# Block-sparse attention into a gated MLP: spatial weights cast in parts, and casts, loads, transposes and splits put elsewhere in the order

## The chip, the cores and the metric

The kernel runs on one core of a Trainium2 chip. The metric is the device time of one execution in microseconds (us); before the change it was 218.19 us, the median of three runs (216.72 to 219.64). The profile is one execution of 218.0 us, with a span of 216.2 us from its first to its last instruction. TensorE had its full clock throughout.

## The reference, cut to what matters

Attention for 4 batches of 8 heads, 768 positions of 64 elements each, under a mask of 32 x 32 blocks (neighbours, first and last blocks, and three sampled ones for each row of blocks). The heads of a batch are joined to rows of 512 and go through a gated MLP whose gate mixes positions by a 768 x 768 matrix, the spatial weights.

```
scores = scale * q @ k.T              # masked by blocks of 32
attn   = softmax(scores)
x      = (attn @ v), heads joined     # [4, 768, 512]
h      = relu(x @ w_in)               # [4, 768, 1024]
u, v   = h[..., :512], h[..., 512:]
v_n    = (v - mean(v)) / sqrt(var(v) + 1e-6)
v_s    = einsum('ts,bsd->btd', w_spatial, v_n) + b_spatial
out    = (u * v_s) @ w_out
```

## The kernel before

**Pairs and slots.** Two heads make a pair; there are 16 pairs (0 to 15), four to a batch. The order of all work is written out by hand, in slots. A slot does one chunk of scores and its exponential: two TensorE matmuls of 384 columns and one ScalarE exponential of 128 x 768. Slots 0 to 47 (`for g in range(N0)`, L672) are batch 0's four pairs, in halves of the queries (`qk_exp_half`, L386, matmuls L396). Then the loop over `p` from 4 to 16 (L728) runs twelve slots `s` for each pair, `g = 12 * p + s` (`qk_exp`, L356, matmuls L361, exponential L365). Behind each slot's scores come one or more matmuls of the MLP (`moe_q.popleft()()`, all through L520) and, seven slots behind the scores, one chunk of attention times values (`av`, L370, matmuls L377; `av_half` with L412 in batch 0). A head that is through is divided by its sums on VectorE (`rc` L442, `xn` L443; L423 and L424 in batch 0) and transposed for the MLP: by a DMA (`xtr`, L466), in batch 0 by TensorE (L433) with a VectorE copy to `xt` (L434).

**What a pair needs.** For pairs from 4 on, `load(p)` (L107) brings q, k and v as floats into `st_q`, `st_k`, `st_v`, two buffers each. `prepare(p)` (L147) casts k, q and v to bf16 on POOL, in that order: `nat_k` and `nat_q` (L140), `vv` (`cast_v`, L143). `tr_dma` (L342, L344) transposes `nat_k` and `nat_q` by DMA into `tt_k` and `tt_q`. `split_pair(p, "k")` and `split_pair(p, "q")` (L347, L350) copy the two heads' halves with VectorE into `kt_all` and `qt_all`, from where the scores read them: two copies of 64 x 768 bf16 for each split. Pair `p`'s splits stand in the slots of pair `p - 1`, its casts and transposes in those of `p - 2`, its loads in those of `p - 3`.

**Queues.** Each engine does its instructions in the order in which this code issues them, and waits for what the instruction at its head needs. All loads, the transposes, and nearly all stores are issued by one DMA queue, SyncE's, in program order too.

**The MLP.** `moe_units(b)` makes the list of a batch: for each of six row chunks, v (`v_post`: relu into `vsb` L533, statistics L536 and L537) and u (`u_post`, L554 or L557); then the mixing product (L520, reading `w_spt` and `vn`; `s_post` makes `gn`, L586, and transposes it by DMA, L590), then the product with `w_out`. After each third v chunk POOL makes `std` (L540) and `rstd` (L542) from the means and variances `mv`, and VectorE then makes `vn` (`normalize`, L547) one chunk at a time, in slots given by `norm_q`. A product's PSUM tile is one of two banks in turn, which its `post` frees.

**The spatial weights.** They come as three loads of 128 x 2 x 768 floats (`load_weights`, L170) and are cast by `cast_weights` (L180, L183) on POOL into `ws_nat`: one instruction for a load, in slot 28 of batch 0, two of them ahead of the loads and weight transposes listed there and one between. In `ws_nat` the order is by chunk, so the cast reads its source with a step of six floats. Six DMA transposes (`wspt`, L472) make `w_spt` of it.

## Time and profile before

| What | Value |
|---|---|
| Time, median of 3 | 218.19 us |
| Span of the profile | 216.2 us |
| Spatial weight casts (L183 POOL) | 3 of 2.97 us, 29.2 to 38.0 us |
| Split copies to `kt_all` (L350 VectorE) | 24, median 356 ns, longest 1929 ns |
| Split copies to `qt_all` (L350 VectorE) | 24, median 355 ns, longest 947 ns |
| POOL waiting for loads of k (L140) | 64.2 us in 11 waits, longest 13.4 us |
| Pair 6's k and q transposes issued | 54.01 and 55.33 us |
| Pair 7's loads issued | 50.28 to 51.76 us |
| Pair 7's k and q transposes issued | 58.20 and 59.52 us |
| Pair 10's loads issued | 83.96 to 85.56 us |
| First product with `w_out` | 82.3 us |

Reading it: a row of a group gives the line of the kernel, the engine, the operation, the tiles by name, and the mean duration; behind it the idle time of that engine before these instructions and what ended it. A row of a timeline gives start and length in us, then the same names, and in brackets the idle time just before it. The chain of waits follows the execution back from its last instruction to whatever released each step. The durations of TensorE's matmuls are modelled, and those of POOL are rough.

The scores of batch 0 run to about 43 us, pair 4's from 42.92 us, pair 5's from about 52 us, pair 6's from 63.87 us. The other pairs follow at 11 to 12 us each, and from about 188 us only batch 3's MLP is left.

### The profile page before, as it was taken

How to read it: one execution, taken by the hardware profiler on the slowest of the kernel's cores; microseconds unless marked ns; L12 is line 12 of the kernel's file. 1: busy time of each engine (PE TensorE's matmuls, PEld its weight loads, DVE VectorE, ACT ScalarE, POOL GpSimd, SP SyncE). 2: the span in 40 equal slices, each digit the busy share in tenths (PEclk: the TensorE clock that was granted, in tenths of full speed). 3: DMA queues.
4: the chain of work that ended last, by engine and by line, in shares of the span. 5: the costliest groups of instructions: out<-in, count | busy, mean ns of one | idle time of the engine just before them, and what ended most of it. 6: DMA issues, size and time to landing. Idle time of an engine off the chain costs nothing.

```text
span 216.2 us, 5234 instructions
## 1 busy us (share of the span) xinstructions
PE 205.8 (95%) x2065; PEld 125.7 (58%) x2099; DVE 132.0 (61%) x311; ACT 172.4 (80%) x238; POOL 69.4 (32%) x97
## 2 busy tenths in 40 slices
PE   8899999999979999999999999999899999999993
PEld 7567766566646666655566565655465656544441
DVE  6777949967454546356957463446978444585542
ACT  7899999899978999998899888888789885266031
POOL 6767979801626121402342400400502000022000
PEclk9999999999999999999999999999999999999999
DMA  5999999979989999999979448989712124620246
GB/s 142 318 338 385 394 325 290 192 125 275 273 229 282 151 244 188 257 287 302 196 181 212 106 83 241 234 168 297 145 19 39 25 52 86 219 101 0 58 120 234
DMA packets 64936, 42.24 MB, mean 195 GB/s; under 512 B 46896, under 2 KB 60560, under 8 KB 64912
## 3 DMA queue, kind: packets, MB, share of 16 engines
q1 hardware_dynamic: 64624, 41.58, 76.2%
q8 instruction: 16, 0.26, 0.5%
q10 hardware_dynamic: 288, 0.33, 0.5%
q14 instruction: 8, 0.07, 0.2%
HBM read 24.38 MB, written 6.29 MB: 142 GB/s over the span
## 4 chain that ended last, share of the span: by engine, by line
PE 82%; DVE 9%; DMA 3%; issue 2%; POOL 1%; ACT 1%; SPq 0%; ACTq 0%; DVEq 0%; POOLq 0%
PE ps_moe L520 32%; PE ps L361 20%; PE ps_av L377 12%; PE ps L396 6%; PE ps_av L412 4%; PE ps_t L520 3%; PE ps_sc L520 3%; DVE kt_all L350 2%; DMA st_k<-in_k_dram 2%; DVE vsb L533 2%; DMA out_dram<-osb 1%; DVE kt_all L277 1%; DVE osb L610 1%; PE ps_av L433 1%; PE ps_moe L322 1%
## 5 line engine op out<-in xcount | busy, mean ns | idle before, releaser
L365 ACT ACTIVATE a_all<-ps 128x768 bf16<-128x768 f32 x144 | 113.4, 813 | 16.5 <-PE ps L361 10.2
L361 PE MATMUL ps<-qt_all,kt_all 88*128 88x384 bf16 x288 | 70.4, 325 | 1.4 <-DVE qt_all L350 1.4
L377 PEld LDWEIGHTS <-a_all 128*128 128x128 bf16 x864 | 46.1, 97 | 34.0 <-issue 1.6
L377 PE MATMUL ps_av<-vv,a_all 128*128 128x65 bf16 x864 | 50.8, 194 | 0.3
L520 PE MATMUL ps_moe<-w_in_t,xt 128*128 128x512 bf16 x143 | 45.2, 378 | 1.9 <-DVE vsb L533 1.0
L400 ACT ACTIVATE a_all<-ps 128x768 bf16<-128x768 f32 x48 | 35.7, 812 | 2.6 <-PE ps L396 2.2
L140 POOL CAST nat_k<-st_k 128x768 bf16<-128x768 f32 (+1 forms) x14 | 10.9, 779 | 73.9 <-DMA st_k<-in_k_dram 64.2
L520 PE MATMUL ps_moe<-vn,w_spt 128*128 128x512 bf16 x110 | 33.1, 379 | 0.3
L586 DVE SCALAR_TENSOR_TENSOR gn<-ps_moe,b_col,un 128x512 bf16<-128x512 f32 x20 | 15.0, 750 | 21.5 <-PE ps_moe L520 17.9
L520 PEld LDWEIGHTS <-xt 128*128 128x128 bf16 x192 | 18.6, 97 | 15.3 <-issue 1.0
L396 PE MATMUL ps<-qt_all,kt_all 88*128 88x384 bf16 x96 | 23.4, 325 | 0.8 <-ACT a_all L400 0.2
L520 PE MATMUL ps_moe<-w_out_t,gt 128*128 128x512 bf16 x73 | 21.5, 378 | 0.3
L520 PEld LDWEIGHTS <-w_spt 128*128 128x128 bf16 x144 | 13.8, 97 | 11.6
L361 PEld LDWEIGHTS <-kt_all 88*128 88x128 bf16 x288 | 19.0, 98 | 2.0 <-DVE qt_all L350 1.5
L412 PEld LDWEIGHTS <-a_all 128*128 128x128 bf16 x288 | 14.9, 98 | 6.3 <-issue 0.9
L533 DVE TENSOR_SCALAR vsb<-ps_moe 128x512 bf16<-128x512 f32 x18 | 12.3, 682 | 10.1 <-PE ps_moe L520 10.0
L536 DVE BATCH_NORM_STATS2 stats<-vsb 128x6 f32<-128x512 bf16 x24 | 16.6, 694 | 1.5 <-ACT vsb L531 0.8
L412 PE MATMUL ps_av<-vv,a_all 128*128 128x65 bf16 x288 | 17.1, 194 | 0.4 <-DVE xt L434 0.4
L540 POOL TENSOR_SCALAR std<-mv 128x3 f32<-128x3 f32 x8 | 1.9, 242 | 42.0 <-DVE mv L537 30.6
L610 DVE COPY osb<-ps_moe 128x512 f32<-128x512 f32 x10 | 6.9, 690 | 13.3 <-PE ps_moe L520 9.8
L443 DVE TENSOR_TENSOR xn<-ps_av,rc 128x384 bf16<-128x384 f32 x24 | 13.4, 557 | 0.8
L520 PEld LDWEIGHTS <-gt 128*128 128x128 bf16 x96 | 8.8, 97 | 7.1
(100 smaller groups left out, 213.1 us busy)
## 6 DMA issues: line engine op xcount, KB each, us to landing
out_dram<-osb SPq DMA_DIRECT2D x23, 256.0 KB, 3.3
st_v<-in_v_dram SPq DMA_DIRECT2D x14, 384.0 KB, 5.5
st_k<-in_k_dram SPq DMA_DIRECT2D x13, 384.0 KB, 4.6
st_q<-in_q_dram SPq DMA_DIRECT2D x12, 384.0 KB, 3.5
wst<-in_moe_w_spatial_dram SPq DMA_DIRECT2D x3, 768.0 KB, 9.4
wst<-in_moe_w_in_dram SPq DMA_DIRECT2D x4, 512.0 KB, 7.7
wst<-in_moe_w_out_dram SPq DMA_DIRECT2D x2, 512.0 KB, 6.3
st_q<-in_q_dram SPq DMA_DIRECT2D x4, 192.0 KB, 6.2
```

The source lines that it names most:

```text
L140: eng.tensor_copy(out=dst, in_=src)
L361: nc.tensor.matmul(out=ps[:, hf * 512:hf * 512 + HALF], lhsT=kt[j % H][:, ci * 128:(ci + 1) * 128], rhs=qt[j % H][:, hf * HALF:(hf + 1) * ...
L365: nc.scalar.activation(out=a_ref[j][:, ci, :].rearrange("p (b c) -> p b c", b=2), in_=ps.rearrange("p (b c) -> p b c", b=2)[:, :, 0:HALF], ...
L377: nc.tensor.matmul(out=av_ref[j][:, qc, :], lhsT=a_ref[j][:, ci, qc * 128:(qc + 1) * 128], rhs=vv[p % NG][:, h, ci, :], start=(ci == 0), s ...
L396: nc.tensor.matmul(out=ps[:, u * 512:u * 512 + HALF], lhsT=kt[j][:, ci * 128:(ci + 1) * 128], rhs=qt[j][:, grp * HALF:(grp + 1) * HALF], s ...
L400: nc.scalar.activation(out=a_ref["half", gh][:, 2 * i:2 * i + 2, :], in_=ps.rearrange("p (b c) -> p b c", b=2)[:, :, 0:HALF], func=AF.Exp, ...
L412: nc.tensor.matmul(out=av_ref["half", gh][:, qc, :], lhsT=a_ref["half", gh][:, ci, qc * 128:(qc + 1) * 128], rhs=vv[p][:, h, ci, :], start ...
L443: nc.vector.tensor_tensor(out=xn_ref[p][:, :, h, :], in0=ps[:, :, 0:D], in1=rc.to_broadcast([128, NCH, D]), op=ALU.mult)
L520: nc.tensor.matmul(out=box[0], lhsT=lhs, rhs=rhs, start=(i == 0), stop=(i == n - 1))
L533: nc.vector.tensor_scalar(out=vsb[:, tcc, :], in0=ps, scalar1=0.0, scalar2=None, op0=ALU.max)
L536: nc.vector.bn_stats(out=stats, in_=vsb[:, tcc, :])
L586: nc.vector.scalar_tensor_tensor(out=gn[:, tcc, :], in0=ps, scalar=b_col[:, tcc:tcc + 1], in1=un[:, tcc, :], op0=ALU.add, op1=ALU.mult)
```

## The change

It moves work in the hand-written order and leaves the computation alone.

1. The three spatial casts are cut into six parts each, of 2 of 6 chunks of one of the two rows: 18 instructions of 128 x 256. VectorE and POOL can then take turns in smaller steps.
2. Pair 4's q split moves from slot 45 to slot 41, which puts its two copies directly behind those of k on VectorE. Pair 5's v cast moves from slot 42 to slot 53 (`p == NG`, `s == 5`), on POOL from ahead of the first `std` and `rstd` to behind them.
3. Around pairs 6 and 7: pair 7's loads go from `s` 9 to 11 of pair 4, so that pair 6's transposes (`s` 10, as before) stand ahead of them in the DMA queue. Pair 6's splits go from `s` 7 and 10 to 6 and 8 of pair 5. Pair 7's casts go from `s` 1 to 7 and its transposes from `s` 6 to 9 of pair 5; on POOL the second `std` and `rstd` now come ahead of them. Pair 8's loads and the two `w_out` loads behind them go from `s` 7 to 10 of pair 5. On the DMA queue, pair 4's `xt` transpose now stands ahead of pair 7's transposes.
4. Pair 10's loads go from `s` 7 to 10 of pair 7, behind a `gt` and an `xt` transpose.
5. Pair 14's splits go from `s` 7 and 10 to 5 and 6 of pair 13: all four copies then stand ahead of a head's `rc` and `xn` on VectorE.

The lists of instructions of TensorE and ScalarE stay as they are.

```diff
             if len(dst.shape) == 4:
                 t = t.rearrange("p a (s c) -> p a c s", c=NCH)
-            w_staged.append((t, dst))
+                w_staged.append([(t[:, i, c:c + 2], dst[:, i, c:c + 2])
+                                 for i in range(2) for c in range(0, NCH, 2)])
+            else:
+                w_staged.append([(t, dst)])
 
     def cast_weights(n):
         for _ in range(n):
-            t, dst = w_staged.popleft()
-            nc.gpsimd.tensor_copy(out=dst, in_=t)
+            for t, dst in w_staged.popleft():
+                nc.gpsimd.tensor_copy(out=dst, in_=t)
...
-        if g in (36, 42):
-            cast_v(4 if g == 36 else 5)
-        if g in (39, 45):
+        if g == 36:
+            cast_v(4)
+        if g in (39, 41):
             split_pair(4, "k" if g == 39 else "q")
...
     for p in range(NG, NP + 1):
+        change = NG < p < NP and p % NG == 0
+
+        splits = {NG: (3, 6), NG + 1: (6, 8), NP - 3: (5, 6)}.get(p, (7, 10))
+        s_prep = {NG: 7, NG + 1: 7}.get(p, 1)
+        s_tr = {NG: 10, NG + 1: 9}.get(p, 8 if change else 6)
+        s_load = {NG: 11, NG + 1: 10, NG + 3: 10}.get(p, 9 if change else 7)
         for s in range(12):
             g = 12 * p + s
-            change = NG < p < NP and p % NG == 0
...
-            if p + 1 < NP and s in ((3, 6) if p == NG else (7, 10)):
-                split_pair(p + 1, "k" if s in (3, 7) else "q")
-            if s == (10 if p == NG else 8 if change else 6) and p + 2 < NP:
+            if p + 1 < NP and s in splits:
+                split_pair(p + 1, "k" if s == splits[0] else "q")
+            if p == NG and s == 5:
+                cast_v(5)
+            if s == s_prep and p + 2 < NP:
+                prepare(p + 2)
+                if p == NG + 2:
+                    cast_weights(2)
+            if s == s_tr and p + 2 < NP:
                 tr_dma(p + 2, "k")
                 tr_dma(p + 2, "q")
-            if s == (7 if p == NG else 1) and p + 2 < NP:
-                prepare(p + 2)
-                if p == 6:
-                    cast_weights(2)
-            if s == (9 if change else 7) and p + 2 < NP:
-                if p + 3 < NP:
-                    load(p + 3)
-                if p == 5:
+            if s == s_load and p + 3 < NP:
+                load(p + 3)
+                if p == NG + 1:
                     load_weights(2)
```

## The prediction

> **What bounds the kernel now.** I read the page's first part, then the chain that ended last, then the timelines of single engines wherever TensorE waited. First the busy times, one engine to a line:
>
> ```profile
> PE 205.8 (95%) x2065; PEld 125.7 (58%) x2099; DVE 132.0 (61%) x311; ACT 172.4 (80%) x238; POOL 69.4 (32%) x97
> PE 82%; DVE 9%; DMA 3%; issue 2%; POOL 1%; ACT 1%; SPq 0%; ACTq 0%; DVEq 0%; POOLq 0%
> ```
>
> TensorE is busy for 205.8 of 216.2 us and holds 82% of the chain. The change leaves TensorE's and ScalarE's lists of instructions as they are, so it can only win time in which TensorE stands still. The start (about 1 us and the first load) and the last output transfer are untouched. Of the rest, TensorE's timeline shows three waits of more than 0.3 us behind VectorE; the bracket is the idle time and what ended it:
>
> ```profile
> 40.88 0.35 PE L412 MATMUL ps_av<-vv,a_all 128*128 128x65 bf16 x6 [0.38 <-DVE xt L434]
> 63.87 0.50 PE L361 MATMUL ps<-qt_all,kt_all 88*128 88x384 bf16 x2 [1.41 <-DVE qt_all L350]
> 154.26 0.59 PE L520 MATMUL ps_moe<-w_in_t,xt 128*128 128x512 bf16 x2 [0.77 <-DVE vsb L533]
> ```
>
> Together 2.56 us. By the starts, instead of the modelled ends, they are somewhat longer. Six L377 matmuls take 0.19 us in the chain, two L361 0.33 us. So TensorE was through at 62.10 + 0.19 = 62.29, and the second wait is 63.87 - 62.29 = 1.58 us. The third is 154.26 - (153.01 + 0.33) = 0.92 us, the first about 0.58 us (VectorE's release at 40.88, the weight load idle for 0.60). This 3.1 us, 1.4% of the time, is what the change can aim at.
>
> The first wait, in the timelines of POOL and VectorE (start, length, instruction), and two pieces of the chain:
>
> ```profile
> 35.02 2.96 POOL L183 CAST ws_nat<-wst 128x1536 bf16<-128x1536 f32 x1
> 36.27 2.30 DVE L350 COPY kt_all<-tt_k 64x768 bf16<-64x768 bf16 x2
> 38.48 0.17 DVE L423 RECIPROCAL rc<-ps_av 128x3 f32<-128x3 f32 x1
> 36.35 1.84 DVE kt_all L350
> 38.21 0.35 DVE kt_all L350
> ```
>
> The same copy takes 0.35 us or 1.9, and the long one ends 0.2 us after POOL's cast. The reciprocal had its input by 37.4 and starts at 38.48. All VectorE work behind it is about 1.1 us late, and TensorE meets that at 40.88.
>
> The second wait:
>
> ```profile
> 57.35 0.83 POOL L140 CAST nat_k<-st_k 128x768 bf16<-128x768 f32 x1 [1.13 <-DMA st_k<-in_k_dram]
> 58.89 0.83 POOL L143 CAST vv<-st_v 128x768 bf16<-128x768 f32 x1
> 59.81 0.23 POOL L540 TENSOR_SCALAR std<-mv 128x3 f32<-128x3 f32 x1
> 61.05 0.41 DVE L547 TENSOR_SCALAR vn<-vsb,mv,rstd 128x512 bf16<-128x512 bf16 x1 [3.12 <-POOL rstd L542]
> 63.47 0.73 DVE L350 COPY qt_all<-tt_q 64x768 bf16<-64x768 bf16 x2
> ```
>
> The statistics mv are there at 57.92, but POOL has pair 7's three casts ahead of std. VectorE idles 3.12 us at its first vn, and pair 6's splits stand behind that vn in its queue.
>
> The third wait:
>
> ```profile
> 151.68 0.83 POOL L140 CAST nat_q<-st_q 128x768 bf16<-128x768 f32 x1
> 152.45 0.95 POOL L143 CAST vv<-st_v 128x768 bf16<-128x768 f32 x1
> 151.79 1.82 DVE L350 COPY kt_all<-tt_k 64x768 bf16<-64x768 bf16 x2
> 153.53 0.67 DVE L533 TENSOR_SCALAR vsb<-ps_moe 128x512 bf16<-128x512 f32 x1
> ```
>
> Pair 14's two k copies take 0.84 and 0.88 us by the chain, each until a POOL cast is over; the vsb behind them frees the bank that TensorE wants.
>
> [...] The trace agrees: 1.84 us beside the 2.96 us cast, and 0.84 and 0.88 us in turn with two casts of 0.83 us. It shows also that POOL gets its turn between two copies (vv took 0.95 instead of 0.83). [...] That fits the spatial casts, whose source steps six floats: 2.97 us for 1536 elements, where the contiguous w_in cast takes 1.04 us for 1024. [...] here casts of 0.83 us start 0.77 us apart, so I take 0.06 us off each.
>
> **The change part by part.**
>
> *Spatial casts in 18 parts instead of 3.* The rows by form give 0.502 us for 384 elements (nat_k, L140) and 0.825 for 768: a slope of 0.84 ns and a fixed 0.18 us. A strided element then costs (2.97 - 0.18)/1536 = 1.82 ns. A part of 256 is 0.18 + 0.47 = 0.65 us, started 0.59 us apart. Eighteen take 10.6 us instead of 8.8, so they end near 39.8, with VectorE's turns near 40.7, instead of 37.98. If the fixed part were hidden altogether a part would cost 0.50 us, and that is the lower bound. Behind them on POOL are pair 5's k and q casts, pair 4's v, then std and rstd. The k cast ends near 41.5; the DMA queue comes to pair 5's k transpose at 41.99 and its q transpose at 44.69. rstd ends near 44.4, the first vn was at 48.77. POOL's extra time is hidden behind the weight transposes (34.28 to 41.89).
>
> *Pair 4's q split moved to slot 41*, directly behind the k split on VectorE. Before, the q copies ran at 41.23 to 42.56, where TensorE did not wait on them. Now four copies stand in a row at 36.27 while POOL is still in its parts, and they should alternate. Each waits for one part and then needs 0.2 us. A turn is 0.7 to 0.85 us, the first one shortened by the part already under way. VectorE is free near 39.2 (38.6 to 39.7) instead of 38.57. So the small parts save 1.5 us on the first copy, and the moved q split takes that and about 0.6 us more. The queue behind it (rc, xn, vsb, stats, mv, xt) is what TensorE waits for at 40.88. I count a loss of 0.6 us, between 0 and 1.1.
>
> *Pair 5's v cast later* (0.83 us, behind the first std and rstd). It frees POOL for std; its reader begins at pair 5's attention, after 60 us. Nothing.
>
> *Pair 6's transposes ahead of pair 7's loads, pair 7's casts six slots later, pair 6's splits at slots 6 and 8.* The second std loses the three casts in front of it: ready at 57.92 + 0.1 + 0.3 + 0.9 = 59.2 instead of 61.02. The k split stands before the first vn; its transpose was issued at 54.01 and lands 2.9 to 4.4 us later, by 58.4. VectorE then does k split to 58.7, vn from 59.2, rc and xn to 60.5, q split to 61.2. TensorE wants it at 62.29, so the wait of 1.58 us goes: 1.5 us won, at least 0.8 if transposes land late.
>
> The price is later loads. Pair 7's are issued near 57.0 instead of 50.28. The k part lands after about 4.0 us (median to landing), the casts end near 63.4 and the q transpose lands near 68. Its k split ran at 70.80 and its q split at 72.47; with 1.5 us won these become 69.3 and 71. Margin 1 to 3 us. The w_out loads start near 67 instead of 62.44; they took up to 9 us, so their casts end near 77.5, and the first product with w_out ran at 82.3. Hidden, by about 3 us.
>
> *Pair 10's loads three slots later*: issued near 87 instead of 83.96. Their casts began at 88.67, their transposes at 93.31, the split is a pair later. Nothing.
>
> *Pair 14's splits at slots 5 and 6.* VectorE idles from 150.04 to 151.09. Four copies of 0.35 us start there; POOL's k cast begins at 150.91, so the first two run free and the last waits to about 152.0. Then rc, xn to 152.9, vsb near 152.95 instead of 153.53. TensorE's wait shrinks from 0.92 to about 0.35: 0.55 us won, between 0 and 0.9.
>
> Sum: +0.6 - 1.5 - 0.55 = -1.45 us, 218.19 to 216.7.
>
> **The rivals.**
>
> *All three waits go.* [...] the four copies are over near 38.1: a gain of 0.4 us at the first place, 1.6 at the second, 0.9 at the third gives 215.3. For it: the 0.06 us overlap of POOL starts. Against: four copies in a row need 4 x 0.35 us even undisturbed, and the cast near 152 shows that POOL takes every second turn.
>
> *The saving is refilled.* TensorE arrives 1.5 us earlier at slots whose transposes and loads are now later, and waits there instead: 218.19 + 0.6 - 0.5 = 218.3. For it: the 1 us margin of pair 7's k split, and VectorE works in order, so a late transpose stops everything behind it. Against: no TensorE wait shows between 64 and 95 us.
>
> *Slower.* The four copies cost the full 1.1 us, pair 7's transposes come late by the longest landing seen for its loads (6.5 us instead of 4.0), eating 1.5 us of the 1.5 won, and the third place wins nothing: 218.19 + 1.1 = 219.3. Speaks for it: all of these bounds come from rows. Against: they would have to fall together.
>
> **How the numbers follow.** I give my forecast 0.55, the larger gain 0.15, the refill 0.18, slower 0.12. The range takes in the larger gain's 215.3 and reaches to just short of the slow case; the three times of before also spread from 216.72 to 219.64. So 215.0 to 219.0. A 2% change would be under 213.8 or over 222.6. All waits that the change touches sum to 3.1 us, less than 4.4, so faster by 2% is 0.03. Slower by 2% needs a new wait of over 4 us, for which I see only the w_out casts: 0.03. The rest, 0.94, is within 2%.
>
> **What would show it.** Right: the wait at L361 near 62 us is gone, with rstd there about 1.8 us earlier; 18 casts of 0.5 to 0.65 us; pair 4's four copies take 2.3 to 3.4 us in all, and the wait on xt L434 grows to around 1 us; pair 14's vsb wait halves. Wrong: the xt wait vanishes (parts cheaper than I think), or a new wait on qt_all near 70 us or on w_out_t near 80 us appears.

## Result and profile after

The changed kernel takes 228.47 us (median of 4 runs, 226.90 to 229.06) against 218.06 us of the kernel before (median over all its runs up to then, 216.72 to 219.64): a ratio of 1.046 (1.037 to 1.055). It is slower by 4.6%. The prediction said 216.7 us and gave a loss over 2% a chance of 0.03, so it was wrong, by the sign and by the size.

The first lines of the page of after: the busy times, then the row of the span in 40 slices that gives TensorE's granted clock in tenths, then the chain's shares.

```profile
span 227.2 us, 5284 instructions
...
PE 211.9 (93%) x2099; PEld 127.5 (56%) x2099; DVE 139.1 (61%) x311; ACT 172.4 (76%) x238; POOL 72.2 (32%) x112
...
PEclk9999999769999999999799999999999999999999
...
PE 70%; DMA 18%; DVE 8%; issue 1%; SPq 1%; POOL 0%; ACT 0%; ACTq 0%; DVEq 0%
```

TensorE has the same list of instructions as before. Its busy time is 6.1 us longer, but the profile of before lacks 34 of the 2099 matmul records (x2065), so this difference can't be read as work that got slower. DMA has 18% of the chain where it had 3%. The clock row dips twice, near 40 to 50 us and near 108 us, which it did nowhere in the profile of before. All four runs of after show it in their mean clock, 0.974 to 0.985.

TensorE's timeline of after has these waits longer than 0.3 us, once the start is over:

```profile
44.89 0.50 PE L437 MATMUL ps_av<-ident,xn 128*128 128x128 bf16 x3 [5.91 <-DVE xn L428]
...
107.16 0.39 PE L524 MATMUL ps_moe<-w_in_t,xt 128*128 128x512 bf16 x1 [3.02 <-DMA xt<-xn]
...
165.22 0.59 PE L524 MATMUL ps_moe<-w_in_t,xt 128*128 128x512 bf16 x2 [0.91 <-DVE vsb L537]
```

The wait of 1.4 us on `qt_all` near 63 us is gone, as intended. In the place of the three small waits stand two large ones and the third as it was. Where the 11.0 us between the spans (227.2 and 216.2) arise is seen best from the slots. This table gives when the exponential of a slot starts, in us from the start of each span:

| Slot | Before | After | After later by |
|---|---|---|---|
| 36 | 33.30 | 33.21 | -0.09 |
| 48 (pair 4) | 43.35 | 50.95 | 7.60 |
| 60 (pair 5) | 52.76 | 60.36 | 7.60 |
| 72 (pair 6) | 64.47 | 70.66 | 6.19 |
| 108 (pair 9) | 95.49 | 101.69 | 6.20 |
| 120 (pair 10) | 107.97 | 118.78 | 10.81 |
| 156 (pair 13) | 144.18 | 155.00 | 10.82 |
| 168 (pair 14) | 157.38 | 168.34 | 10.96 |

So 7.6 us are lost ahead of slot 48, 1.4 are won between 60 and 72 (predicted: 1.5), 4.6 are lost between 108 and 120, and elsewhere the two profiles move apart by less than 0.2 us.

**The first loss.** POOL's and VectorE's timelines of after, around pair 4's splits (start, length, instruction):

```profile
30.14 10.56 POOL L187 CAST ws_nat<-wst 128x256 bf16<-128x256 f32 x18 [1.02 <-DMA wst<-in_moe_w_spatial_dram]
40.64 0.84 POOL L140 CAST nat_k<-st_k 128x768 bf16<-128x768 f32 x1
41.41 0.84 POOL L140 CAST nat_q<-st_q 128x768 bf16<-128x768 f32 x1
42.18 0.84 POOL L143 CAST vv<-st_v 128x768 bf16<-128x768 f32 x1
46.47 0.23 POOL L544 TENSOR_SCALAR std<-mv 128x3 f32<-128x3 f32 x1 [3.45 <-DVE mv L541]
```

```profile
36.62 6.61 DVE L354 COPY kt_all<-tt_k 64x768 bf16<-64x768 bf16 x1 [0.37 <-DMA tt_k<-nat_k]
...
43.63 0.72 DVE L354 COPY qt_all<-tt_q 64x768 bf16<-64x768 bf16 x2
44.27 0.17 DVE L427 RECIPROCAL rc<-ps_av 128x3 f32<-128x3 f32 x1
44.47 0.36 DVE L428 TENSOR_TENSOR xn<-ps_av,rc 128x192 bf16<-128x192 f32 x1
```

A copy of 0.35 us takes 6.61 us. It starts during the 12th of the 18 casts (at 36.59) and ends at 43.23, 0.21 us after POOL's last cast (42.18 + 0.84 = 43.02). It had no turn after the 12th cast nor after any of the eight after that; it went when POOL ran out of work. The three other copies, behind the row, take 0.35 us each. `rc` and `xn` behind them are what TensorE waits 5.91 us for. The windows of after over that stretch (columns from the third: TensorE busy, weight loads, VectorE, ScalarE, POOL, then the granted clock; the last two are of the DMA):

```profile
40.00:44.00 4.00, 0.00 (x0) 0.00 (x0) 3.94 (x4) 0.00 (x0) 3.02 (x5) 0.88 1.15 282
44.00:48.00 4.00, 3.11 (x22) 1.89 (x23) 2.96 (x9) 1.35 (x2) 1.45 (x3) 0.50 0.77 148
48.00:52.00 4.00, 4.00 (x40) 2.48 (x39) 1.23 (x3) 2.93 (x5) 0.46 (x1) 0.76 1.04 130
```

After the wait TensorE runs at half its clock: the trace has 0.5 from 43.06 us for 6.83 us. The work goes on at 44.89, so 5.0 us of it run at half the clock, which I estimate to cost 2.5 us. Together 5.9 + 2.5 = 8.4 us, less the wait of 0.6 that was there before: 7.8, near the 7.6 in the table.

**The second loss.** The DMA queue's own timeline of after, and of before, up to the same `xt` transpose, that of pair 7:

```profile
97.38 0.57 SPq L110 DMA_DIRECT2D st_q<-in_q_dram  x1
...
99.07 2.12 SPq L615 DMA_DIRECT2D out_dram<-osb  x4
101.28 2.88 SPq L470 DMA_TRANSPOSE xt<-xn  x1
```

```profile
83.96 0.57 SPq L110 DMA_DIRECT2D st_q<-in_q_dram  x1
...
88.40 3.24 SPq L611 DMA_DIRECT2D out_dram<-osb  x4
92.00 1.22 SPq L466 DMA_TRANSPOSE xt<-xn  x1
```

Before, this transpose was issued 3.5 us ahead of slot 108 (95.49 - 92.00); now 0.4 us ahead (101.69 - 101.28). It is 3.1 us later against TensorE's work, and TensorE waits 3.02 us for it. The clock is half for 3.41 us from 107.91, all of it in work: 1.7 us by the same estimate. The sum is 4.7, near the 4.6 in the table.

In the profiles of this case half the clock followed all single waits of TensorE of over 2 us (2.14 to 5.91 us) but one (2.37 us, without), and came at two places with less (a wait of 1.82 us, and two of 1.03 and 1.01 us close together); waits of 1.1 to 1.7 us went without it. In after the stretches at half clock are 6.83 and 3.41 us long; what sets their start and their length, no run shows. It is not certain to come: of four runs of one kernel below, three had a mean clock of 0.981 to 0.985 and took 222.71 to 223.71 us, and the fourth had its full clock and took 220.22.

### The profile page after: what moved, and what is told of

The parts are those of the page before. It is cut to its first block, busy times and chain, and to the rows that moved or that the text cites. A ratio compares the mean times of both kernels' runs of the same rounds, so it can differ in the third digit from the quotient of the medians.

```text
span 227.2 us, 5284 instructions
## 1 busy us (share of the span) xinstructions
PE 211.9 (93%) x2099; PEld 127.5 (56%) x2099; DVE 139.1 (61%) x311; ACT 172.4 (76%) x238; POOL 72.2 (32%) x112
## 4 chain that ended last, share of the span: by engine, by line
PE 70%; DMA 18%; DVE 8%; issue 1%; SPq 1%; POOL 0%; ACT 0%; ACTq 0%; DVEq 0%
PE ps_moe L524 31%; PE ps L365 19%; PE ps_av L381 11%; DMA wst<-in_v_dram 4%; DMA tt_k<-nat_k 4%; DVE kt_all L354 4%; DMA st_q<-in_q_dram 4%; PE ps_t L524 3%; PE ps_sc L524 3%; DMA xt<-xn 3%; DMA st_v<-in_v_dram 2%; DVE vsb L537 1%; DVE qt_all L354 1%; PE ps L400 1%; PE ps_av L416 1%
## 5 line engine op out<-in xcount | busy, mean ns | idle before, releaser
L365 PE MATMUL ps<-qt_all,kt_all 88*128 88x384 bf16 x288 | 70.9, 327 | 0.0
L381 PEld LDWEIGHTS <-a_all 128*128 128x128 bf16 x864 | 46.5, 98 | 34.3 <-issue 2.4
L524 PE MATMUL ps_moe<-w_in_t,xt 128*128 128x512 bf16 x160 | 51.7, 389 | 4.1 <-DMA xt<-xn 3.0
L381 PE MATMUL ps_av<-vv,a_all 128*128 128x65 bf16 x864 | 51.2, 194 | 0.0
L524 PE MATMUL ps_moe<-vn,w_spt 128*128 128x512 bf16 x120 | 35.6, 378 | 0.0
L400 PE MATMUL ps<-qt_all,kt_all 88*128 88x384 bf16 x96 | 24.7, 341 | 0.5 <-ACT a_all L404 0.2
L524 PE MATMUL ps_moe<-w_out_t,gt 128*128 128x512 bf16 x80 | 23.0, 378 | 0.0
L537 DVE TENSOR_SCALAR vsb<-ps_moe 128x512 bf16<-128x512 f32 x18 | 12.3, 683 | 14.8 <-PE ps_moe L524 14.7
L416 PEld LDWEIGHTS <-a_all 128*128 128x128 bf16 x288 | 15.6, 100 | 6.5 <-issue 1.5
L416 PE MATMUL ps_av<-vv,a_all 128*128 128x65 bf16 x288 | 17.6, 197 | 0.0
L354 DVE COPY kt_all<-tt_k 64x768 bf16<-64x768 bf16 x24 | 15.7, 655 | 0.6 <-DMA tt_k<-nat_k 0.4
L614 DVE COPY osb<-ps_moe 128x512 f32<-128x512 f32 x10 | 6.9, 690 | 13.3 <-PE ps_moe L524 13.3
```

Source lines behind the costliest of these rows:

```text
L354: nc.vector.tensor_copy(out=(qt if nm == "q" else kt)[(2 * p + h) % H][0:D, :], in_=src[h * D:(h + 1) * D, :])
L365: nc.tensor.matmul(out=ps[:, hf * 512:hf * 512 + HALF], lhsT=kt[j % H][:, ci * 128:(ci + 1) * 128], rhs=qt[j % H][:, hf * HALF:(hf + 1) * ...
L381: nc.tensor.matmul(out=av_ref[j][:, qc, :], lhsT=a_ref[j][:, ci, qc * 128:(qc + 1) * 128], rhs=vv[p % NG][:, h, ci, :], start=(ci == 0), s ...
L400: nc.tensor.matmul(out=ps[:, u * 512:u * 512 + HALF], lhsT=kt[j][:, ci * 128:(ci + 1) * 128], rhs=qt[j][:, grp * HALF:(grp + 1) * HALF], s ...
L416: nc.tensor.matmul(out=av_ref["half", gh][:, qc, :], lhsT=a_ref["half", gh][:, ci, qc * 128:(qc + 1) * 128], rhs=vv[p][:, h, ci, :], start ...
L524: nc.tensor.matmul(out=box[0], lhsT=lhs, rhs=rhs, start=(i == 0), stop=(i == n - 1))
```

## The experiments

The times of a group of runs are compared with those of the kernel before on the same chip, and ratios have 95% intervals. From group to group compare the ratios, not the times: the median of the kernel before was 217.23 to 219.60 us. Where a copy's cast is counted, the count starts behind the last point at which POOL had to wait for something; in the bare rows the one-element cast that does this waiting is left out. In the diffs `...` stands between pieces that lie apart.

### Which part of the change costs what

**The parts alone.** The kernel before, with the 18 small casts and nothing else of the change:

```diff
-            w_staged.append((t, dst))
+                w_staged.append([(t[:, i, c:c + 2], dst[:, i, c:c + 2])
+                                 for i in range(2) for c in range(0, NCH, 2)])
...
-            nc.gpsimd.tensor_copy(out=dst, in_=t)
+            for t, dst in w_staged.popleft():
+                nc.gpsimd.tensor_copy(out=dst, in_=t)
```

> The kernel before with the spatial casts in 18 parts and nothing else. 'Starved': one k copy takes 4 to 7 us, TensorE waits 4 to 6 us near 41 us and gets half its clock after it: 224 to 227 us, no wait on xt near 100 us. Rival 'q split' (four copies in a row cause it): 217 to 219 us.

Measured: 223.83 us, ratio 1.024 (1.016 to 1.031). VectorE's and TensorE's timelines of this kernel:

```profile
36.04 7.31 DVE L353 COPY kt_all<-tt_k 64x768 bf16<-64x768 bf16 x1
```

```profile
44.26 0.50 PE L436 MATMUL ps_av<-ident,xn 128*128 128x128 bf16 x3 [5.60 <-DVE xn L427]
```

The long copy needs neither the moved q split nor anything else of the change. It starts in the 12th cast again and ends 0.21 us after the last of POOL's row, at 43.35. The wait of TensorE and the 6.83 us at half clock come with it.

**All but the parts.** The changed kernel with the three casts whole:

```diff
-                w_staged.append([(t[:, i, c:c + 2], dst[:, i, c:c + 2])
-                                 for i in range(2) for c in range(0, NCH, 2)])
+                w_staged.append([(t, dst)])
```

> The changed kernel with the three spatial casts whole again, all other edits kept. Theory 'starved' (VectorE's first k copy of pair 4 gets no turn between POOL's short parts): the copy falls from 6.6 us to under 2 us, TensorE's wait at 45 us from 5.9 to under 1.5 us, the half clock behind it goes, and the time is 219 to 222 us; the wait on xt near 105 us stays at about 3 us with its half clock. Rival 'late transpose' (the stall is pair 4's k transpose landing late, or the q split put directly behind): the stall stays over 4 us and the time over 226 us.

Measured: 222.72 us, ratio 1.018 (1.011 to 1.026). The first k copy takes 1.77 us, and slot 48 starts at 44.20 us instead of 43.35: 0.85 us, the cost of the q split directly behind the k split (the four copies end at 39.41, and `xn` comes after). Slots 60 to 72 take 10.29 us instead of 11.71: the 1.4 us are won without the parts too. The second loss stays, and is larger. TensorE's timeline of this kernel:

```profile
101.39 0.61 PE L523 MATMUL ps_moe<-w_in_t,xt 128*128 128x512 bf16 x1 [4.02 <-DMA xt<-xn]
```

So the parts make the first loss, by themselves, and something among the other edits makes the second. The order in the DMA queue is the suspect.

**Pair 10's loads back at their slot**, in the changed kernel, and once more with the casts whole as well:

```diff
-        s_load = {NG: 11, NG + 1: 10, NG + 3: 10}.get(p, 9 if change else 7)
+        s_load = {NG: 11, NG + 1: 10}.get(p, 9 if change else 7)
```

> The changed kernel with pair 10's loads three slots earlier again, as before. Theory 'load 10' (these 1.2 MB stand directly ahead of four stores and pair 7's xt transpose in the DMA queue): the 3.0 us wait on xt and the half clock behind it go, 223 to 225 us. Rival 'whole queue' (pairs 7 and 8's later casts and loads have put all of the DMA queue behind by 4 us, load 10 is only one link): the wait stays over 2 us, 226 to 229 us.

> Both undone: casts whole, pair 10's loads as before. If 'starved' and 'load 10' are both right: 215.5 to 217.5 us, a little under the kernel before, by the 1.4 us wait near 63 us. If 'whole queue' is right: 219 to 221 us, with the xt wait still there.

Measured: 227.32 us, ratio 1.038 (1.030 to 1.046), and with the casts whole 222.94, ratio 1.015 (1.003 to 1.027). TensorE's timelines of the first and of the second:

```profile
101.70 0.39 PE L524 MATMUL ps_moe<-w_out_t,gt 128*128 128x512 bf16 x1 [2.14 <-DMA gt<-gn]
```

```profile
96.86 0.61 PE L523 MATMUL ps_moe<-w_out_t,gt 128*128 128x512 bf16 x1 [2.34 <-DMA gt<-gn]
```

The second profile is of the longest of its four runs (223.71 us). The wait on `xt` is gone in both: pair 10's loads did put it there. But another takes its place, on the last `gt` of batch 0, of 2.1 to 2.3 us. The idea that these loads alone made the second loss fell. My reading was that the queue had been late since pair 7, and that the loads only choose which transpose TensorE meets late.

### Where the queue became late

The DMA queue of after, earlier on:

```profile
58.62 0.47 SPq L110 DMA_DIRECT2D st_v<-in_v_dram  x1
68.56 1.22 SPq L470 DMA_TRANSPOSE xt<-xn  x1
69.87 1.23 SPq L348 DMA_TRANSPOSE tt_k<-nat_k  x1
71.19 1.24 SPq L348 DMA_TRANSPOSE tt_q<-nat_q  x1
72.48 0.89 SPq L110 DMA_DIRECT2D st_q<-in_q_dram  x1
...
74.44 1.30 SPq L175 DMA_DIRECT2D wst<-in_moe_w_out_dram  x2
75.86 3.56 SPq L594 DMA_TRANSPOSE gt<-gn  x2
```

For 9.5 us nothing is issued: at the head stands pair 4's `xt`, whose `xn` VectorE makes at 67.97 to 68.53. Behind it stand pair 7's transposes, pair 8's loads, `w_out` and the first `gt`. Before, all but the `gt` had gone out ahead of that `xt`:

```profile
63.53 1.31 SPq L466 DMA_TRANSPOSE xt<-xn  x1
66.50 4.42 SPq L590 DMA_TRANSPOSE gt<-gn  x2
```

Against slot 72 the first two `gt` are issued 5.2 us later (75.86 - 70.66) and were 2.0 us later before (66.50 - 64.47). Of these 3.2 us, 1.4 come from slot 72 itself, which TensorE reaches that much earlier.

**Pair 8's and the `w_out` loads back at their slot** (with the casts whole and pair 10's loads back):

```diff
-        s_load = {NG: 11, NG + 1: 10}.get(p, 9 if change else 7)
+        s_load = {NG: 11, NG + 1: 7}.get(p, 9 if change else 7)
```

> The run with the casts whole and pair 10's loads early, and now pair 8's loads and the w_out loads at slot 7 of pair 5 as before, so that they stand ahead of pair 4's xt and pair 7's transposes in the DMA queue. Theory 'queue order' (the queue stands still in front of pair 4's xt transpose until its xn is made, with these loads behind it): the gt transposes start 3 us earlier and the 2.3 us wait on gt near 97 us and its half clock go: 217.5 to 220 us. Rival (the late gt comes from pair 7's casts behind std on POOL alone): the wait stays over 1 us, 221.5 to 224 us.

Measured: 219.09 us, ratio 1.013 (1.002 to 1.024), hardly under the 1.015 without this edit. The wait on `gt` is 1.10 us instead of 2.1 to 2.3, and no half clock follows it. But the first `gt` are not issued earlier, as was expected: 5.6 us after slot 72 (69.97 - 64.38), and 5.5 without the edit (71.55 - 66.02).

**Pairs 6 and 7 alone.** The kernel before with the edits around pairs 6 and 7 and the later v cast: casts whole, pair 10's loads, the q split and pair 14's splits as before. Then the same with pair 8's and the `w_out` loads back. Against the changed kernel with whole casts and pair 10's loads back, the first of the two is:

```diff
-        if g in (39, 41):
+        if g in (39, 45):
...
-        splits = {NG: (3, 6), NG + 1: (6, 8), NP - 3: (5, 6)}.get(p, (7, 10))
+        splits = {NG: (3, 6), NG + 1: (6, 8)}.get(p, (7, 10))
```

> The kernel before with the edits around pairs 6 and 7 alone (pair 7's loads and casts later, pair 6's splits earlier, pair 8's and the w_out loads later, pair 5's v cast later). Theory: the 1.4 us wait near 63 us goes (1.5 us won), and a wait of 2 to 4 us on gt or xt near 97 to 101 us with half clock after it comes: 218.5 to 222 us, slower than before by 0 to 3 us. Rival 'they only won': 216 to 217.5 us.

> The run above with pair 8's and the w_out loads left at slot 7. If the DMA queue's order is the whole cause of the wait near 97 us, only the win at 63 us is left: 1.0 to 1.8 us under the kernel before, the fastest of all; else as e_pairs67.

Measured: 219.82 us, ratio 1.011 (1.003 to 1.020), and 220.37, ratio 1.014 (1.007 to 1.022). Both lose the wait near 63 us. Both get one on `gt` near 94 us instead: 2.37 and 1.74 us. The loads that I put back were not the whole of it; pair 7's transposes still stood behind `xt`. The DMA queue of the first:

```profile
58.06 0.47 SPq L110 DMA_DIRECT2D st_v<-in_v_dram  x1
60.35 1.21 SPq L469 DMA_TRANSPOSE xt<-xn  x1
...
68.90 3.33 SPq L593 DMA_TRANSPOSE gt<-gn  x2
```

Here the queue stands still for only 1.8 us ahead of `xt`, and yet the first `gt` come 6.0 us after slot 72 (68.90 - 62.93). So most of the 9.5 us above is the first loss, by which `xn` came late, and the length of this stop is not what makes the `gt` late.

**Pair 7's transposes ahead of `xt`, and the loads nearly where they were.** Pair 7's loads are at `s` 9 of pair 4, two slots later than in the kernel before (its code has them at 7, so the change moved them from 7 to 11, not from 9 as the list of the change says), ahead of pair 6's transposes again; pair 8's and the `w_out` loads are at their old slot. In the second kernel pair 10's loads are late again, as here:

```diff
-        s_tr = {NG: 10, NG + 1: 9}.get(p, 8 if change else 6)
-        s_load = {NG: 11, NG + 1: 7}.get(p, 9 if change else 7)
+        s_tr = {NG: 10, NG + 1: 8}.get(p, 8 if change else 6)
+        s_load = {NG: 9, NG + 1: 7, NG + 3: 10}.get(p, 9 if change else 7)
```

> The edits around pairs 6 and 7 without the later loads: pair 6's splits at slots 6 and 8, pair 7's casts behind std at slot 7, its transposes at slot 8 ahead of pair 4's xt, pair 5's v cast behind std; all loads as before, casts whole. Theory 'queue order': no DMA is later than before except pair 7's transposes by about 2 us, so the wait at 63 us goes and the one on gt near 94 us is under 0.8 us: 1 to 2 us under before. Rival 'DMA bound' (from 50 to 100 us the DMA engines have no slack, so TensorE gives back at gt whatever it wins at 63 us): within 0.5 us of before.

> The same with pair 10's loads at slot 10 of pair 7, behind the last gt transpose, as in the changed kernel. 'Queue order': the last gt lands earlier and the gt wait is gone, but xt of pair 7 comes later: a wait on xt near 99 us of 0 to 2 us; between 1.5 us under before and 1 us over. 'DMA bound': a wait of over 2 us on xt.

Measured: 218.29 us, ratio 1.001 (0.997 to 1.005), and 217.91, ratio 0.9985 (0.9955 to 1.0015). The DMA queue of the second:

```profile
57.46 0.98 SPq L175 DMA_DIRECT2D wst<-in_moe_w_out_dram  x2
60.48 1.21 SPq L347 DMA_TRANSPOSE tt_k<-nat_k  x1
61.80 1.23 SPq L347 DMA_TRANSPOSE tt_q<-nat_q  x1
63.54 1.27 SPq L469 DMA_TRANSPOSE xt<-xn  x1
65.50 4.43 SPq L593 DMA_TRANSPOSE gt<-gn  x2
```

The first two `gt` come 2.3 us after slot 72 (65.50 - 63.17). In this profile TensorE waits neither near 63 us nor on `gt` or `xt`; its largest wait between 45 and 150 us is 0.27 us. Pair 7's casts still stand behind the second `std` and pair 6's splits are still early, so neither of these made the second loss: the order of the queue's entries around pairs 6 to 8 did. Two things were put back in one step, pair 7's transposes and its loads, and which of them counts was not separated. The profile of the first kernel, one of its longest runs (220.47 us), still has a wait of 1.03 us on `qt_all` at 64.19 and one of 1.01 on `vn` at 65.92, none on `gt` or `xt`. Neither kernel is faster than the one before.

Pair 10's late loads cost nothing here (0.9985 with them, 1.001 without), as predicted for them: they hurt where the queue behind them is late already.

### Why a waiting copy got no turn

The prediction took it that POOL and VectorE take turns, one instruction each. In the traces above the copy had none for 5.3 to 7.3 us. So I tried turns in bare rows of casts, without the kernel.

> Leaves the whole computation out (its output is zeros) and measures the disputed wait by itself: POOL runs a row of casts, and VectorE sends two 64 x 768 copies into it at nine different moments (five for the first kind). Four kinds of row: 'long' 6 casts of 768 contiguous elements, 'short' 12 of 256 contiguous, 'strided' 12 of 256 with a step of six floats as in the changed kernel, 'waiting' the same strided casts, each waiting for the end of the one ahead. Theory 'closed row' (VectorE gets no turn as long as POOL's next instruction has nothing to wait for): the first copy takes until the end of the row in long, short and strided, 2 to 6 us, and under 1 us in waiting. Theory 'short parts' (only short or strided instructions close up): under 1.1 us in long and waiting, 2 to 6 us in strided. Theory 'turns' (my prediction: a turn after each POOL instruction): under 1.1 us in all, so that the stall of the changed kernel would have another cause.

Here VectorE's delay ahead of the copies was a memset, and it kept POOL out: the one-element cast ahead of the row, 0.19 us in the kernels below, took 1.44, 1.61 and 1.78 us in the first three rows, with memsets of 1.06, 1.19 and 1.32 us beside it and a copy of 0.29 us behind them. So the first of each two copies ran ahead of the row, and the second arrived at the row's first cast and had its turn after it. That tells nothing of later casts.

> Leaves the whole computation out (output zeros), as the run before it; now the delay ahead of VectorE's two copies is made of copies out of PSUM, so that they arrive 0.5 to 5 us into POOL's row (in the run before they all came at its first cast, and the second copy had its turn after one cast). Theory 'closed row': a copy that arrives when the following casts are already on their way, with nothing to wait for, gets no turn before the last of them: up to 5 us in long, short and strided, under 1 us in waiting. Theory 'turns': under 1.1 us everywhere.

With a delay that copies from PSUM the arrivals spread from the first to the 11th cast. Every copy had its turn after the cast under way, with at most 0.90 us beside casts of 128x768, 0.60 beside short ones and 0.79 beside strided ones. "A row without a gap keeps VectorE out" fell as a general rule.

**A break after every part**, in the kernel with the parts alone: a one-element POOL copy that reads what the part wrote, and so waits for it.

```diff
                 nc.gpsimd.tensor_copy(out=dst, in_=t)
+                if len(dst.shape) == 3 and dst.shape[-1] == 128:
+                    nc.gpsimd.tensor_copy(out=note, in_=dst[:, 0, 0:1])
```

> The kernel before with the 18 short casts, each followed by a one-element POOL copy that reads its result and so has to wait for it (4 us more on POOL). 'Closed row': VectorE's k copies of pair 4 take under 1.2 us each instead of 7.3, TensorE's wait near 44 us falls from 5.6 to under 1 us and its half clock goes: 216.5 to 219.5 us against 223.8 for the same parts without the waits. 'Turns', or a cost of short strided casts as such: still 223 us or more.

Measured: 222.43 us, ratio 1.020 (1.010 to 1.030). The two k copies take 0.63 and 0.83 us, and the wait near 44 us is gone. The row itself is now late: the parts start 0.83 us apart, and pair 5's `nat_k` is cast from 44.50 us instead of 39.98 (4.5 us later, not the 2 us that one of the expectations below gives). TensorE waits 1.18 us on `xn` at 49.37 and 3.15 us on `qt_all` at 66.45, with half clock behind the second. The turns are there, but the time did not come down as expected.

What differed between the bare rows and the kernel was open: the DMA and ScalarE work beside them, or the number of casts that had run. The next four runs tell these apart.

> A kernel of its own that leaves the whole computation out: rows of 26 strided casts of 128x256 on POOL, each row with two VectorE copies of 64x768 arriving near the 5th, 10th, 13th and 16th cast; first alone (plain), then with four loads, eight DMA transposes and twelve ScalarE exponentials beside them (traffic), last with the copies reading a tile that a DMA transpose has just written (wait). Theory 'row' (a long unbroken row on POOL keeps VectorE out by itself): the copies that arrive after the 10th cast take several us, to the end of the row, in the plain rows too. Theory 'traffic' (DMA and ScalarE work beside it is needed): plain copies take 0.35 to 0.8 us, those with traffic several us. If all copies take under 1 us, neither is the cause and what differs in the kernel stays open.

POOL's and VectorE's timelines of this bare kernel, for a copy arriving in the fifth cast and for one in the tenth, with nothing beside them:

```profile
9.32 15.20 POOL L99 CAST parts<-src 128x256 bf16<-128x256 f32 x26
...
24.94 14.95 POOL L99 CAST parts<-src 128x256 bf16<-128x256 f32 x26
```

```profile
11.82 0.65 DVE L114 COPY c_out<-c_in 64x768 bf16<-64x768 bf16 x1
...
30.35 9.79 DVE L114 COPY c_out<-c_in 64x768 bf16<-64x768 bf16 x1
```

The same copy takes 0.65 us in the one row and 9.79 in the other, where it ends 0.21 us after POOL's last instruction. All the arrivals, plain and with traffic:

| Cast under way | Plain | With DMA and ScalarE work |
|---|---|---|
| 5th, 6th | 0.65, 0.69 us | 0.66, 0.70 us |
| 10th | 9.79 us | 9.84 us |
| 12th | 8.35 us | 8.39 us |
| 16th | 6.21 us | 6.18 us |
| 18th and 19th, copies behind a DMA transpose | | 5.42, 4.65 us |

Traffic makes no difference, nor does the copy's own wait for a DMA. In these rows what counts is how far the row has run when the copy arrives, in casts or in time.

**Half the parts.** The kernel before with each spatial cast in two. The edit against the kernel with the parts alone:

```diff
-                w_staged.append([(t[:, i, c:c + 2], dst[:, i, c:c + 2])
-                                 for i in range(2) for c in range(0, NCH, 2)])
+                w_staged.append([(t[:, i], dst[:, i]) for i in range(2)])
```

> The kernel before with each spatial cast in 2 parts of 128x768 instead of 6 of 128x256. The row of POOL work is as long in time, but has 6 instructions and not 18. Theory 'number' (many short instructions in a row keep VectorE out): pair 4's first k copy gets a turn within one cast, at most 1.8 us, and the time is that of before within 0.5%. Theory 'row' (any unbroken row does): the copy takes 5 us or more, to the end of POOL's row near 43 us, and the time is 4 to 5 us above before, as with 18 parts.

Measured: 217.41 us, ratio 0.998 (0.996 to 1.001). POOL and VectorE of this kernel:

```profile
28.93 9.29 POOL L185 CAST ws_nat<-wst 128x768 bf16<-128x768 f32 x6 [1.02 <-DMA wst<-in_moe_w_spatial_dram]
```

```profile
36.00 0.79 DVE L352 COPY kt_all<-tt_k 64x768 bf16<-64x768 bf16 x1
36.80 1.64 DVE L352 COPY kt_all<-tt_k 64x768 bf16<-64x768 bf16 x1
```

The copies arrive 7 us into the row, as in the kernel with 18 parts (36.04 - 29.45 = 6.6), and each has its turn after the cast under way, the fifth and the sixth. So it is not the time that POOL has been busy. What is left is the number of instructions, or their being short.

**One break, and one after every third part.** The one-element copy behind the ninth part only (shown), and behind each third; `n` counts the parts of a load:

```diff
...
+                if len(w_staged) == 1 and n == 2 and len(dst.shape) == 3:
+                    nc.gpsimd.tensor_copy(out=note, in_=dst[:, 0, 0:1])
```

> The kernel before with 18 parts and one such break only, behind the 9th part, two or three parts ahead of the copy's arrival. Theory 'index' (what matters is how many casts have run without a break when the copy arrives): as in the bare rows with up to ten casts ahead, the copy gets a turn after one cast, under 1.5 us. Theory 'row' (what matters is that no break follows): 5 us or more, to the end of POOL's row.

> The kernel before with 18 parts and a one-element POOL copy, which waits for the part ahead of it, behind every third part (6 in all; 18 of them freed VectorE but made POOL's row 2 us longer). If any break gives VectorE its turn: the first k copy takes at most 2 us (up to three parts of 0.6), the row ends within 0.7 us of that without breaks, and the time is that of before within 1%. If only a break right behind each part does: 5 us or more again.

With one break, POOL and VectorE:

```profile
30.49 5.34 POOL L187 CAST ws_nat<-wst 128x256 bf16<-128x256 f32 x9 [1.03 <-DMA wst<-in_moe_w_spatial_dram]
35.90 0.19 POOL L189 COPY note<-ws_nat 128x1 bf16<-128x1 bf16 x1
36.03 5.70 POOL L187 CAST ws_nat<-wst 128x256 bf16<-128x256 f32 x9
```

```profile
37.05 0.41 DVE L356 COPY kt_all<-tt_k 64x768 bf16<-64x768 bf16 x1 [0.63 <-DMA tt_k<-nat_k]
37.47 0.71 DVE L356 COPY kt_all<-tt_k 64x768 bf16<-64x768 bf16 x1
```

A single wait of POOL, ahead of the copy's arrival, brings the turns back: 0.41 and 0.71 us, in the second and third cast after it, with no break behind. With six breaks they are 0.34 and 0.70 us. The time with one was 219.84 us (a single run), with six 219.72, ratio 1.006 (1.002 to 1.011). POOL's row ends 3.3 and 3.8 us later than with half parts (44.94 and 45.45, against 41.64; it also began 1.6 and 0.9 us later), and TensorE waits 2.3 and 3.4 us on `qt_all` near 65 us, with half clock behind it. That the second comes of the first was not followed up.

**How many casts it takes.** The bare rows once more, with other casts and counts:

> A kernel of its own that leaves the whole computation out: rows of casts on POOL with two VectorE copies arriving after more or fewer of them: strided casts of 128x256 (26 in a row, arrivals near the 8th, 9th and 10th), contiguous casts of 128x768 (15 in a row, near the 8th, 9th and 11th), contiguous casts of 128x256 (26 in a row, near the 10th, 12th and 16th), and a strided row with one POOL memset behind the 7th cast that waits for nothing (arrival near the 10th). Theory 'count' (about ten instructions back to back and the next ones are no longer given up): in every kind the copies under nine get a turn within 1 us and those above ten go to the end of the row; the memset changes nothing, because it is no wait. Theory 'short instructions': only rows of 128x256 casts do it, the 128x768 row gives a turn at the 11th too.

Strided casts: turns of 0.59 to 0.82 us at the 8th to 11th cast. Contiguous 128x768: turns of 0.40 to 1.08 us at the 8th to 11th. Contiguous 128x256: turns of 0.44 to 0.48 us at the 10th to 13th, and 3.81 us, to the end of the row, at the 16th. The expected sharp limit of ten did not show. A strided row gave a turn at the tenth cast here and gave none at the tenth in the two rows above, with the copy about 0.2 us into the cast each time. In the trial with a memset in the row the copy arrived at the tenth too, and so it tells nothing of the memset. Rows of the longer casts were not tried beyond the 11th, so whether the shortness of the casts matters as well as their number stays open.

**The good parts together**: the kernel in which no wait had come in place of the one near 63 us (0.9985), with each spatial cast in two.

```diff
-                w_staged.append([(t, dst)])
+                w_staged.append([(t[:, i], dst[:, i]) for i in range(2)])
```

> The kernel before with pair 6's splits at slots 6 and 8 of pair 5, pair 7's casts at slot 7 and its transposes at slot 8 (ahead of pair 4's xt), all loads where they were but pair 10's three slots later, and each spatial cast in 2 parts of 128x768. If the waits near 41 and 63 us are both gone and nothing comes in their place: 1.5 us and about 0.3 us less, ratio 0.992. If something refills them: 0.998 to 1.002, as with either change alone (0.9985 and 0.9984).

Measured: 217.85 us, ratio 1.002 (0.998 to 1.005). That is the outcome named for a refill, not the 0.992. Its profile has a span of 214.7 us, 1.5 less than that of before at the start of this text, but runs of the kernel before on the same chip had spans from 214.5 us on. The wait near 63 us is gone, that at 41 us is 0.34 (0.38 before). One reason was seen: the kernel with half parts has the order of before around pair 6, and its profile has 0.58 us at the place where that of before had 1.41. So the wait near 63 us isn't the same size in every execution, and the profile that the prediction rested on had a large one. Whether that accounts for all of the missing gain is open.

## Why the prediction was wrong

**The cost of a part: right.** The 18 casts start 0.59 us apart and take 0.65; the row took 10.56 us (predicted 10.6), and ended at 40.7 (39.8).

**"Now four copies stand in a row at 36.27 while POOL is still in its parts, and they should alternate": wrong, and the largest error.** I had seen POOL and VectorE alternate in rows of two or three casts (0.84 and 0.88 us for two copies), and carried it over to a row of 18. The copy arrived at the 12th cast, and POOL gave no turn until its row of work ended, 6.6 us later. `xn` stood behind the copies, and TensorE waited 5.9 us for it. The four copies took 7.7 us in all, where 2.3 to 3.4 were named. That a copy waits only for the cast under way, the runs show in short rows (0.79 and 1.64 us for two copies in the row of six casts); who comes next when a long row stands behind that cast, the profile of before did not show, and the alternation there was my estimate. Whether POOL's extra time would have been hidden, as the prediction says, the changed kernel does not show, because TensorE was already 7.6 us late behind the row. In the kernels with breaks, whose rows end later still, TensorE waits 2.3 to 3.4 us near 65 us.

**The q split: "a loss of 0.6 us, between 0 and 1.1": right in one profile, low in others.** With whole casts slot 48 starts 0.85 us later, in two more profiles with the same edit 1.3 and 3.0 us; in the last one half clock followed the 1.82 us wait on `xn`. Within the changed kernel the k copy hides it.

**Pair 6's order: right.** The second `rstd` is ready 6.54 us after slot 60 instead of 8.26 (1.7 us earlier, predicted 1.8), and 1.4 us are won there against the 1.5 predicted. That the size fits is in part luck: with the old order around pair 6, slots 60 to 72 took 11.71 us in the profile of before, but 10.88 with half parts.

**"Margin 1 to 3 us" and "Hidden, by about 3 us" for the later loads: wrong.** I followed the loads to their casts and to the readers of those casts, and these did have the time. I did not follow the queue to what stood behind them. The change put `xt` of pair 4 ahead of pair 7's transposes, and everything behind it waited for an `xn`; the first `gt` came 3.2 us later against the slots, and TensorE met the late transposes 25 to 40 us on, at the end of batch 0's MLP and the start of batch 1's: 3.02 us of waiting on `xt`, 4.6 us with the clock. The list of the change even names the new order. The rival of the refill had a part of it, late transposes that TensorE meets earlier, but looked for it at once and gave it at most 1.5 us. Neither of the two places named as signs of being wrong, `qt_all` near 70 us and `w_out_t` near 80 us, had a wait.

**"Pair 10's loads three slots later: nothing": wrong in this kernel**, because they stand ahead of four stores and of pair 7's `xt`. It was right in the queue that is not late (0.9985).

**The clock: missing from the prediction.** Both long waits (5.91 and 3.02 us) were followed by half the granted clock (0.5), for 5.0 and 3.4 us of work, by the estimate above 4.2 us of loss in all. A long wait was priced at its length alone.

**Pair 14's splits: "0.55 us won, between 0 and 0.9": not shown.** VectorE's timeline of after has the four copies ahead of `rc` and `xn`, 3.1 us in all, and TensorE's wait there is 0.91 us. From slot 156 to 168 the profiles with the new slots take 12.3 to 13.3 us, those with the old ones 12.5 to 13.2.

The sum by the table, 7.6 - 1.4 + 4.6 + 0.1, is 10.9 of its 10.96 us. The range was too narrow, because both its ends came from costs that I could name, and a chance of 0.03 for a new wait over 4 us took in only one place in which such a wait could arise.

## What to carry to other kernels

Cutting a long GpSimd instruction into many small ones doesn't by itself give VectorE more turns: here a copy of 0.35 us that met the 12th of 18 short casts run back to back took 6.61 us, to the end of POOL's row. So cut into few pieces (beside six casts two copies took 0.79 and 1.64 us); a wait of POOL shortly before the copy arrives gave the turns back too (0.34 and 0.70 us with six such waits), but cost time of its own here (ratio 1.006, against 0.998 with six casts and no wait). When an entry in an in-order DMA queue is moved, walk the queue on from there and ask of every later entry when its reader needs it; the ones that hurt here were met 25 to 40 us on. And price a long TensorE wait with the stretch at half clock that may follow it: here 5.0 and 3.4 us of work after waits of 5.91 and 3.02 us.

## What the runs showed that I had not expected

- A VectorE copy of 64x768 bf16 that meets a row of POOL casts has its turn after the cast under way when that is the ninth of the row or an earlier one (0.34 to 1.1 us beside casts of up to 0.83 us), and goes to the end of the row (up to 9.8 us) when it is the twelfth or a later one of the strided casts (for contiguous 128x256: a turn at the 13th, none at the 16th). Between these the runs differ. A wait of POOL ahead of the copy's arrival brought the turns back (0.41 and 0.71 us). What keeps VectorE out in the longer rows, no run shows.
- When the copy goes at last, it ends 0.21 us after POOL's last instruction, in the kernel as in most bare rows; in three of them it went ahead of the last instruction, a memset.
- A VectorE memset of f32 kept POOL out as well: a one-element cast of 0.19 us took 1.44 us and more when a memset of 1.06 us or more began 0.13 us or more after it, with a copy of 0.29 us behind the memset.
- A row of 26 strided casts with two turns in it took 15.20 us, one with none 14.95: about 0.13 us for each turn.
